# Head sums of six token groups: from selector matmuls on TensorE to copies between SBUF partitions and adds on VectorE

## The chip, the cores and the metric

The kernel runs on one core of one Trainium2 chip. The metric is the time of one execution on the device in microseconds (us). A profiled execution also has a span, from the first to the last instruction, which is about 1.7 us shorter than the time of the same execution. Each profile shows the mean TensorE clock that the chip granted; 1.000 is full speed.

## The reference, cut to what matters

Two layers run over 2048 tokens of width 1024. Each layer has a layer norm, a sliding, dilated attention, a residual, a second layer norm, a dense network with a GELU, and a second residual. The attention has 32 heads of 32 channels; every token looks at itself and at seven earlier tokens, two apart. For each token, head and offset the score is a sum over 32 channels:

```
for offset w in 0..7:
    score[token, head, w] = sum over 32 channels of q[token, head, :] * k[token - 2*(7 - w), head, :]
weights = softmax(score * 32**-0.5)      # over the 8 offsets
out[token, head, :] = sum over w of weights[w] * v[token - 2*(7 - w), head, :]
```

The kernel cuts the tokens into groups of 512. Two layers of four groups make eight groups, numbered 0 to 7. It works as a pipeline: while TensorE does the dense layers of group n, VectorE does the attention of a later group.

Of the kernel before, what the change touches and what calls it, by code (L numbers as in the profile page):

```python
# [9 lines left out]
ALU = mybir.AluOpType  # L10
AX = mybir.AxisListType
BF16 = mybir.dt.bfloat16
F32 = mybir.dt.float32
# [4 lines left out]
def kernel(  # L18
# [18 lines left out]
    P = 128  # L37
    _, S, D = A_x.shape
    F = B_w1.shape[1]
    H = 32  # L40
    DH = D // H
    W = 8
    DIL = 2
    HALO = (W - 1) * DIL
# [3 lines left out]
    T = 512  # L48
    NTT = T // P
# [4 lines left out]
    HP = P // H  # L54
# [18 lines left out]
    bigp = ctx.enter_context(tc.tile_pool(name="bigp", bufs=3))  # L73
    dram = ctx.enter_context(tc.tile_pool(name="dram", bufs=2, space=bass.MemoryType.DRAM))
    smp = ctx.enter_context(tc.tile_pool(name="smp", bufs=1))
# [28 lines left out]
    vec, act, pool, sp = InOrder(nc.vector), InOrder(nc.scalar), InOrder(nc.gpsimd), InOrder(nc.sync)  # L104
# [12 lines left out]
    def mm(*args, **kwargs):  # L117
        return pe(nc.tensor.matmul(*args, **kwargs))  # L118
# [113 lines left out]
    def ln_first():  # L232

        xa[0] = new_xnT()
        vec.on = True
        both = psum.tile([P, 2, KD, P], BF16, name="L", bufs=1)
        stats = {}
# [24 lines left out]
    def win(t_ap):  # L262
        a = t_ap.ap
        assert len(a) == 2 and a[1][0] == 1 and a[1][1] == HALO + T
        return bass.AP(tensor=t_ap.tensor, offset=t_ap.offset, ap=[list(a[0]), [DIL, W], [1, T]])

    st = {n: {} for n in range(N)}
    xa = {}
    xb = {}
# [9 lines left out]
    def head_sum(n, last=True):  # L279

        if "L" not in st[n]:
            st[n]["L"] = psum.tile([P, W, P], F32, name="L", bufs=1)
            start = True
        else:
            start = False
        L = st[n]["L"]
        prod = st[n]["prods"].pop(0)
        for wh in range(2):
            for tb in range(NTT):
                mm(L[tb * H:(tb + 1) * H, wh * 4:(wh + 1) * 4, :], lhsT=smat[:],  # L290
                   rhs=prod[:, wh * 4:(wh + 1) * 4, tb * P:(tb + 1) * P], start=start,
                   stop=last, skip_group_check=True, tile_position=(0, tb * H))

    def new_prod(n, c):

        s = st[n]
        prod = bigp.tile([P, W, T], BF16, name="big")
        vec.tensor_tensor(out=prod[:], in0=s["qT"][:, c, :].unsqueeze(1).to_broadcast([P, W, T]), in1=win(s["kT"][:, c, :]), op=ALU.mult)
        tree = s["prods"]
        tree.append(prod)  # L300
        if c % 2 == 1:
            for _ in range(1 if c % (NCH // s["parts"]) == 1 else 2):
                b = tree.pop()
                vec.tensor_tensor(out=tree[-1][:], in0=tree[-1][:], in1=b[:], op=ALU.add)

    def gen_qkv(n, parts=1, defer=False, qk_pool=None, v_late=False, qk_next=None):
# [46 lines left out]
        if g + 1 < NG:  # L353
            act.copy(vhalo[:], vT[:, :, T:T + HALO])

    def attend(n):

        s = st[n]
        head_sum(n)
        L = s.pop("L")  # L360
        if n % NG == 0:
            vec.tensor_tensor(out=L[0:H, 0:W - 1, 0:HALO], in0=L[0:H, 0:W - 1, 0:HALO], in1=mask[:], op=ALU.add)
        mx = smp.tile([P, P], F32, name="mx")
        vec.tensor_reduce(out=mx[:], in_=L[:].rearrange("p w t -> p t w"), axis=AX.X, op=ALU.max)
        e = smp.tile([P, W, P], F32, name="e")
        vec.tensor_tensor(out=e[:], in0=L[:], in1=mx[:].unsqueeze(1).to_broadcast([P, W, P]), op=ALU.subtract)
        act.activation(e[:], e[:], ACT.Exp, scale=SCALE)
        z = smp.tile([P, P], F32, name="z")
        vec.tensor_reduce(out=z[:], in_=e[:].rearrange("p w t -> p t w"), axis=AX.X, op=ALU.add)
        vec.reciprocal(z[:], z[:])  # L370
        a = smp.tile([P, W, P], BF16, name="a")
        vec.tensor_tensor(out=a[:], in0=e[:], in1=z[:].unsqueeze(1).to_broadcast([P, W, P]), op=ALU.mult)
        s["a"] = a
# [45 lines left out]
    def gen_ffn1(n):  # L419
        xnT = xb.pop(n)  # L420
        hT = hpool.tile([P, KF, T], BF16, name="hT")
        st[("h", n)] = hT
        for j4 in range(KF // 4):
            wt = wpool.tile([P, KD, 4 * P], BF16, name="wt")
            sp.dma_start(wt[:], w1_v[:, :, j4 * 4 * P:(j4 + 1) * 4 * P])
            for jj in range(4):
                j = j4 * 4 + jj
                ps = acc_tile()
                for k in range(KD):
                    mm(ps[:], lhsT=wt[:, k, jj * P:(jj + 1) * P], rhs=xnT[:, :, k, :], start=(k == 0), stop=(k == KD - 1))  # L430
                act.activation(hT[:, j, :], ps[:], ACT.Gelu_apprx_tanh, bias=b1T[:, j:j + 1])
                yield

    def gen_ffn2(n):
        l, g = divmod(n, NG)
        hT = st.pop(("h", n))
        for dh in range(2):
            cols = slice(dh * HALF, (dh + 1) * HALF)
            xb2 = None
            if n == N - 1:  # L440
                xb2 = bigp.tile([P, NTT, HALF], F32, name="big")
                for tt in range(NTT):
                    vec.tensor_tensor(out=xb2[:, tt, :], in0=x[g * NTT + tt][:, cols], in1=b2bc[:, cols], op=ALU.add)

            parts = [[slice(0, HALF)] for _ in range(NTT)]
            if n == N - 1 and dh == 1:
                parts[-1] = [slice(0, HALF // 2), slice(HALF // 2, HALF)]
            pss = [[acc_tile() for _ in p] for p in parts]
            for kq in range(4):
                wt = wpool.tile([P, KQ, HALF], BF16, name="wt")  # L450
                sp.dma_start(wt[:], w2_v[:, kq * KQ:(kq + 1) * KQ, cols])
                for tt in range(NTT):
                    t = g * NTT + tt
                    for ps, cs in zip(pss[tt], parts[tt]):
                        ps = ps[:, 0:cs.stop - cs.start]
                        for k in range(KQ):
                            mm(ps, lhsT=hT[:, kq * KQ + k, tt * P:(tt + 1) * P], rhs=wt[:, k, cs],
                               start=(kq == 0 and k == 0), stop=(kq == 3 and k == KQ - 1))
                        if kq < 3:
                            continue  # L460
                        out_cols = slice(dh * HALF + cs.start, dh * HALF + cs.stop)
                        xs = x[t][:, out_cols]
                        if xb2 is not None:
                            vec.tensor_tensor(out=xs, in0=ps, in1=xb2[:, tt, cs], op=ALU.add)
                        else:
                            tmp = iop.tile([P, HALF], F32, name="tmp")
                            vec.tensor_tensor(out=tmp[:], in0=ps, in1=b2bc[:, out_cols], op=ALU.add)
                            vec.tensor_tensor(out=xs, in0=tmp[:], in1=xs, op=ALU.add)
                        if l == NLAYER - 1:
                            sp.dma_start(out_v[t * P:(t + 1) * P, out_cols], xs)  # L470
                    yield
# [24 lines left out]
    def stage(gen, count=None, sides=()):  # L496


        u = 0
        while count is None or u < count:  # L500
            if next(gen, gen) is gen:
                break
            for v, f in sides:
                if v == u:
                    f()
            u += 1
        for v, f in sides:
            if v >= u:
                f()

    def at(u, f, *args, **kwargs):
        return [(u, lambda: f(*args, **kwargs))]

    def each(f, n, u0, du, c0=0, c1=NCH):
        return [(int(u0 + du * (c - c0)), lambda c=c: f(n, c)) for c in range(c0, c1)]

    hold = vec.hold
# [14 lines left out]
        stage(q2, sides=each(new_prod, 1, 0, 1, 4, 8) + at(4, transpose_late))  # L532
    hpool = ctx.enter_context(tc.tile_pool(name="hpool", bufs=1))
    stage(gen_ffn1(0), sides=at(4, attend, 1) + at(4, spread, 1) + at(4, hold) + each(new_prod, 2, 2, 1, 0, 4) + each(av, 1, 6, 2))
    stage(gen_ffn2(0), sides=at(0, ln_stats_ahead, 3) + at(15, hold) + each(new_prod, 2, 15, 1, 4, 8) + at(23, hold) + at(23, ln_a, 3, None, True))
    for n in range(1, N - 2):
        stage(gen_wo(n), sides=at(0, spread, n + 1) if n > 1 else at(7, attend, 2))
        stage(gen_qkv(n + 2), sides=(at(0, spread, 2) if n == 1 else []) + each(av, n + 1, 0, 2, 0, 3))
        stage(gen_ffn1(n), sides=at(20 if n == 1 else 9, attend, n + 2) + each(av, n + 1, 8, 2, 3, 8))
        if n + 3 < N:  # L540
            stage(gen_ffn2(n), sides=at(2, ln_a, n + 3))
        else:
            stage(gen_ffn2(n), sides=at(0, spread, n + 2) + each(av, n + 2, 1, 4))
    n = N - 2
# [35 lines left out]
```

## The kernel before: the parts that the change and the argument touch

Every instruction of VectorE (DVE), ScalarE (ACT), GpSimd (POOL) and of the weight-load queue is issued through one helper, which the profile therefore names as line L93. All matmuls but the transposes go through `mm`, line L118.

```python
    class InOrder:
        def __getattr__(self, name):
            f = getattr(self.engine, name)
            def call(*args, **kwargs):
                inst = f(*args, **kwargs)                     # L93
                ...                                           # cut: optional order against earlier ones
                return inst
            return call
        def hold(self):                                       # what comes later stays behind what was issued so far
            self.floor = self.last

    vec, act, pool, sp = InOrder(nc.vector), InOrder(nc.scalar), InOrder(nc.gpsimd), InOrder(nc.sync)
    def mm(*args, **kwargs):
        return pe(nc.tensor.matmul(*args, **kwargs))          # L118; `pe` keeps program order
```

TensorE and POOL keep program order. The order of VectorE, ACT and the weight-load queue is chosen when the program is built, apart from the `hold` calls; once built, it is fixed. Six accumulators `acc` in PSUM take the results of TensorE (`bufs=6`); `big` has three buffers.

The 32 channels of a head lie four to a chunk in eight chunks. `new_prod` multiplies q and k for a chunk and VectorE adds the chunks up pairwise, until one product of 128 partitions (32 heads x 4 channels), 8 offsets and 512 tokens is left. `head_sum` adds the last four partitions of each head: a selector matrix `smat` of ones does it on TensorE, in eight matmuls of 128x32, and puts 128-token blocks under each other, so that `L` has (block, head) on the partitions. `attend` does the softmax.

```python
    def head_sum(n, last=True):
        ...
        for wh in range(2):
            for tb in range(NTT):                             # NTT = 4 token blocks, H = 32 heads
                mm(L[tb * H:(tb + 1) * H, wh * 4:(wh + 1) * 4, :], lhsT=smat[:],
                   rhs=prod[:, wh * 4:(wh + 1) * 4, tb * P:(tb + 1) * P], ...)

    def new_prod(n, c):
        prod = bigp.tile([P, W, T], BF16, name="big")
        vec.tensor_tensor(out=prod[:], in0=q of chunk c, in1=win(k of chunk c), op=ALU.mult)   # shortened
        ...                                                   # cut: pairwise adds

    def attend(n):
        head_sum(n)
        L = s.pop("L")
        ...
        vec.tensor_reduce(out=mx[:], in_=L[:].rearrange("p w t -> p t w"), axis=AX.X, op=ALU.max)
        e = smp.tile([P, W, P], F32, name="e")
        vec.tensor_tensor(out=e[:], in0=L[:], in1=mx[:].unsqueeze(1).to_broadcast([P, W, P]), op=ALU.subtract)
        act.activation(e[:], e[:], ACT.Exp, scale=SCALE)
        vec.tensor_reduce(out=z[:], in_=e[:].rearrange("p w t -> p t w"), axis=AX.X, op=ALU.add)
        ...                                                   # cut: reciprocal, a = e * 1/z

    # in gen_qkv, before the V chunks are written:
        act.copy(vT[:, :, 0:HALO], (zhalo if g == 0 else vhalo)[:])      # vT has bufs=2
    # in gen_ffn1, 28 times:
                act.activation(hT[:, j, :], ps[:], ACT.Gelu_apprx_tanh, bias=b1T[:, j:j + 1])
    # the layer norm of the next group, four times: rows to columns by a transposing DMA
        sp.dma_start_transpose(xnT[:, tt, :, :], xn[:].rearrange("s (k p) -> s k p", p=P))
```

The driver issues the stages in this order; `at(u, f)` calls `f` after output tile `u` of the stage.

```python
    stage(gen_ffn2(0), sides=... + at(23, hold) + at(23, ln_a, 3, None, True))
    for n in range(1, N - 2):
        stage(gen_wo(n), sides=at(0, spread, n + 1) if n > 1 else at(7, attend, 2))
        stage(gen_qkv(n + 2), sides=...)
        stage(gen_ffn1(n), sides=at(20 if n == 1 else 9, attend, n + 2) + each(av, n + 1, 8, 2, 3, 8))
        ...                                                   # cut: ffn2 of n, layer norm of n + 3
```

## Time and profile before

| | before |
|---|---|
| time | 1239.21 us median of 3 runs (1239.06 to 1240.82) |
| span of the profiled run, granted clock | 1237.2 us, 1.000 |
| TensorE (PE) busy | 1231.2 us |
| VectorE (DVE) busy | 840.0 us, 68% |
| waits of PE after 150 us | none over 0.45 us |

These are lines of the page of the kernel before: busy time with share of the span, the chain of work that ended last by engine, and the issues of one kind of copy (number, size of each, median us from issue to landing).

```profile
PE 1231.2 (100%) x5841; PEld 632.9 (51%) x5841; DVE 840.0 (68%) x868; ACT 306.3 (25%) x477; POOL 94.3 (8%) x214
...
PE 97%; DVE 1%; POOL 1%; DMA 0%; issue 0%; ACT 0%
...
abc<-a_d POOLq DMA_DIRECT2D x32, 256.0 KB, 4.6
```

PE works nearly the whole time and the chain that decides the end is PE. So only two things can move the time: fewer instructions on PE, or new waits of PE.

### The profile page before, as it was taken

The numbers are of one execution on the slowest core, as the hardware profiler recorded it, in microseconds if no ns is written. First come the engines' busy times: TensorE is split into PE (matmuls) and PEld (weight loads), VectorE is DVE, ScalarE is ACT, GpSimd is POOL, SyncE is SP. The second block draws the span as 40 slices with busy tenths as digits, with TensorE's granted clock in tenths as the row PEclk, the third lists the DMA queues.
The fourth block names the chain that finished last, engine by engine and source line by source line (L and its number), as shares of the span: only waits on it lengthen the run. The fifth ranks groups of instructions, "written<-read, shape, count | busy, mean of one in ns | idle before, by whom it ended". The sixth has DMA issues, their size and how long they took to land.

```text
span 1237.2 us, 14039 instructions
## 1 busy us (share of the span) xinstructions
PE 1231.2 (100%) x5841; PEld 632.9 (51%) x5841; DVE 840.0 (68%) x868; ACT 306.3 (25%) x477; POOL 94.3 (8%) x214
## 2 busy tenths in 40 slices
PE   9999999999999999999999999999999999999998
PEld 6666544456444564445644455444654444444444
DVE  7989899996985899337994379843597788012001
ACT  4333252023420144101341023510235001300310
POOL 4010210012000100001000010100001002000000
PEclk9999999999999999999999999999999999999999
DMA  9954564576646555656556565566654568556441
GB/s 308 279 179 146 165 198 161 168 176 216 191 156 201 161 177 161 196 168 183 170 157 198 172 182 160 164 198 199 171 170 135 184 200 193 169 157 195 152 136 53
DMA packets 215327, 219.81 MB, mean 178 GB/s; under 512 B 66066, under 2 KB 184992, under 8 KB 212192
## 3 DMA queue, kind: packets, MB, share of 16 engines
q1 hardware_dynamic: 212592, 208.16, 54.7%
q0 software_dynamic: 2672, 10.76, 2.8%
q8 instruction: 45, 0.74, 0.2%
q14 instruction: 18, 0.15, 0.0%
HBM read 197.40 MB, written 6.29 MB: 165 GB/s over the span
## 4 chain that ended last, share of the span: by engine, by line
PE 97%; DVE 1%; POOL 1%; DMA 0%; issue 0%; ACT 0%
PE acc L118 97%; POOL rstd L93 1%; DVE stats L93 1%; PE L L118 0%; DVE x L93 0%; DMA x<-in_A_x_dram 0%; DVE xn L93 0%; DVE big L93 0%; PE acc L211 0%; DVE mv L93 0%; PE L L211 0%; ACT xnT L93 0%
## 5 line engine op out<-in xcount | busy, mean ns | idle before, releaser
L118 PE MATMUL acc<-xnT,wt 128*128 128x512 bf16 (+1 forms) x3376 | 721.7, 376 | 0.6 <-ACT xnT L93 0.6
L118 PEld LDWEIGHTS <-wt 128*128 128x128 bf16 x3376 | 398.6, 119 | 320.9 <-issue 3.9
L118 PE MATMUL acc<-wt,hT 128*128 128x512 bf16 (+1 forms) x1820 | 388.1, 376 | 0.0
L118 PEld LDWEIGHTS <-hT 128*128 128x128 bf16 x1820 | 178.1, 98 | 209.0
L93 DVE TENSOR_TENSOR big<-big 128x1024 bf16<-128x1024 bf16 (+2 forms) x184 | 244.2, 1359 | 1.8
L93 ACT ACTIVATE hT<-acc,b1T 128x512 bf16<-128x512 f32 x224 | 151.8, 687 | 319.8 <-PE acc L118 319.2
L93 DVE TENSOR_TENSOR big<-abc,vT 128x4096 bf16<-128x4096 bf16 x64 | 144.0, 2283 | 49.3 <-DMA abc<-a_d 49.3
L93 DVE TENSOR_TENSOR tmp<-acc,b2bc 128x512 f32<-128x512 f32 x56 | 38.6, 690 | 180.9 <-PE acc L118 177.4
L93 DVE TENSOR_TENSOR big<-qT,kT 128x4096 bf16<-128x4096 bf16 x64 | 143.8, 2285 | 23.7 <-ACT kT L93 23.1
L93 ACT CAST qT<-acc 128x512 bf16<-128x512 f32 x64 | 37.4, 586 | 329.2 <-PE acc L118 329.2
L118 PE MATMUL acc<-wt,oT 128*128 128x512 bf16 x448 | 97.9, 379 | 0.0
L93 DVE BATCH_NORM_STATS2 stats<-x 128x6 f32<-128x512 bf16 x128 | 83.7, 679 | 3.3 <-DMA x<-in_A_x_dram 2.7
L118 PEld LDWEIGHTS <-oT 128*128 128x128 bf16 x448 | 43.8, 98 | 52.9 <-issue 0.2
L93 DVE TENSOR_TENSOR x<-acc,big 128x512 bf16<-128x512 f32 (+1 forms) x9 | 5.7, 633 | 90.0 <-PE acc L118 90.0
L93 ACT CAST vT<-acc 128x512 bf16<-128x512 f32 x64 | 37.5, 586 | 83.7 <-PE acc L118 83.7
L93 POOL TENSOR_TENSOR rstd<-mv,eps_t 128x1 f32<-128x1 f32 x60 | 18.5, 308 | 502.3 <-DVE mv L93 502.3
L93 ACT CAST kT<-acc 128x512 bf16<-128x512 f32 x64 | 37.5, 586 | 71.7 <-PE acc L118 71.7
L93 POOL DMA_DIRECT2D a_d<-a x32 | 19.0, 620 | 410.7 <-DVE a L93 410.7
L93 DVE TENSOR_SCALAR xn<-x,mv,rstd 128x1024 bf16<-128x1024 bf16 x52 | 28.6, 550 | 30.0 <-POOL rstd L93 29.5
L93 DVE TENSOR_TENSOR x<-acc,x 128x512 bf16<-128x512 f32 x64 | 43.0, 672 | 6.1 <-PE acc L118 5.8
L93 DVE TENSOR_TENSOR x<-tmp,x 128x512 bf16<-128x512 f32 x56 | 38.6, 690 | 1.5
L93 POOL TENSOR_TENSOR rstd<-rstd,mhalf 128x1 f32<-128x1 f32 x60 | 33.9, 565 | 4.7
(54 smaller groups left out, 211.3 us busy)
## 6 DMA issues: line engine op xcount, KB each, us to landing
wt<-in_B_w_dram SPq DMA_DIRECT2D x56, 1024.0 KB, 5.5
wt<-in_B_w_dram SPq DMA_DIRECT2D x64, 896.0 KB, 4.7
wt<-in_A_wqkv_dram SPq DMA_DIRECT2D x46, 1024.0 KB, 5.6
wt<-in_A_wo_dram SPq DMA_DIRECT2D x16, 1024.0 KB, 4.9
abc<-a_d POOLq DMA_DIRECT2D x32, 256.0 KB, 4.6
x<-in_A_x_dram SPq DMA_DIRECT2D x16, 256.0 KB, 5.4
out_dram<-x SPq DMA_DIRECT2D x31, 128.0 KB, 1.8
wt<-in_A_wqkv_dram SPq DMA_DIRECT2D x4, 512.0 KB, 6.8
```

The lines of the kernel that those rows point to most:

```text
L93: inst = f(*args, **kwargs)
L118: return pe(nc.tensor.matmul(*args, **kwargs))
```

## The change

The intent is to take six of the eight head sums off PE, the engine that bounds the kernel, and to put them on engines with room. Groups 0 and 1 keep the matmuls.

```diff
@@ new_prod: the product is laid out by token block
-        prod = bigp.tile([P, W, T], BF16, name="big")
-        vec.tensor_tensor(out=prod[:], in0=..., in1=win(s["kT"][:, c, :]), op=ALU.mult)
+        prod = bigp.tile([P, NTT, W, P], BF16, name="big")
+        q = s["qT"][:, c, :].rearrange("p (b t) -> p b t", t=P)
+        vec.tensor_tensor(out=prod[:], in0=q.unsqueeze(2).to_broadcast([P, NTT, W, P]), in1=win_by_tile(s["kT"][:, c, :]), op=ALU.mult)
@@ new
+    def gather(n):
+        s = st[n]
+        prod = s["prods"].pop(0)
+        Lq = bigp.tile([P, HP, W, P], BF16, name="big")
+        s["Lq"] = Lq
+        for tb in range(NTT):
+            pool.dma_start(Lq[tb * H:(tb + 1) * H, :, :, :], prod[:, tb, :, :])
@@ attend
-        head_sum(n)
-        L = s.pop("L")
+        e = smp.tile([P, W, P], F32, name="e")
+        if "Lq" in s:
+            Lq = s.pop("Lq")
+            vec.tensor_tensor(out=e[:], in0=Lq[:, 0, :, :], in1=Lq[:, 1, :, :], op=ALU.add)
+            for j in range(2, HP):
+                vec.tensor_tensor(out=e[:], in0=e[:], in1=Lq[:, j, :, :], op=ALU.add)
+            L = e
+        else:
+            head_sum(n)
+            L = s.pop("L")
@@ driver
-    stage(gen_ffn2(0), sides=... + at(23, hold) + at(23, ln_a, 3, None, True))
+    stage(gen_ffn2(0), sides=... + at(23, hold) + at(23, gather, 2) + at(23, ln_a, 3, None, True))
         stage(gen_qkv(n + 2), ...)
+        gather(n + 2)
         stage(gen_ffn1(n), ...)
```

Each of the four copies of a group reads all 128 partitions and writes 32 of them: the four channels of a head, which lay on four partitions, come to lie side by side on one.

More of the change, by code (lines that the diff above doesn't have):

```diff
@@ L265, in win, with win_by_tile @@
         return bass.AP(tensor=t_ap.tensor, offset=t_ap.offset, ap=[list(a[0]), [DIL, W], [1, T]])
+    def win_by_tile(t_ap):
+        a = t_ap.ap
+        assert len(a) == 2 and a[1][0] == 1 and a[1][1] == HALO + T
+        return bass.AP(tensor=t_ap.tensor, offset=t_ap.offset, ap=[list(a[0]), [P, NTT], [DIL, W], [1, P]])
     st = {n: {} for n in range(N)}
@@ L290, in head_sum @@
                 mm(L[tb * H:(tb + 1) * H, wh * 4:(wh + 1) * 4, :], lhsT=smat[:],
-                   rhs=prod[:, wh * 4:(wh + 1) * 4, tb * P:(tb + 1) * P], start=start,
+                   rhs=prod[:, tb, wh * 4:(wh + 1) * 4, :], start=start,
                    stop=last, skip_group_check=True, tile_position=(0, tb * H))
@@ L296, in new_prod @@
         s = st[n]
-        prod = bigp.tile([P, W, T], BF16, name="big")
-        vec.tensor_tensor(out=prod[:], in0=s["qT"][:, c, :].unsqueeze(1).to_broadcast([P, W, T]), in1=win(s["kT"][:, c, :]), op=ALU.mult)
+        prod = bigp.tile([P, NTT, W, P], BF16, name="big")
+        q = s["qT"][:, c, :].rearrange("p (b t) -> p b t", t=P)
+        vec.tensor_tensor(out=prod[:], in0=q.unsqueeze(2).to_broadcast([P, NTT, W, P]), in1=win_by_tile(s["kT"][:, c, :]), op=ALU.mult)
         tree = s["prods"]
@@ L364, in attend @@
         vec.tensor_reduce(out=mx[:], in_=L[:].rearrange("p w t -> p t w"), axis=AX.X, op=ALU.max)
-        e = smp.tile([P, W, P], F32, name="e")
         vec.tensor_tensor(out=e[:], in0=L[:], in1=mx[:].unsqueeze(1).to_broadcast([P, W, P]), op=ALU.subtract)
@@ L534 @@
     stage(gen_ffn1(0), sides=at(4, attend, 1) + at(4, spread, 1) + at(4, hold) + each(new_prod, 2, 2, 1, 0, 4) + each(av, 1, 6, 2))
-    stage(gen_ffn2(0), sides=at(0, ln_stats_ahead, 3) + at(15, hold) + each(new_prod, 2, 15, 1, 4, 8) + at(23, hold) + at(23, ln_a, 3, None, True))
+    stage(gen_ffn2(0), sides=at(0, ln_stats_ahead, 3) + at(15, hold) + each(new_prod, 2, 15, 1, 4, 8) + at(23, hold) + at(23, gather, 2) + at(23, ln_a, 3, None, True))
     for n in range(1, N - 2):
```

## The prediction

> **What bounds the kernel now.** TensorE. The page gives PE 1231.2 us busy of a 1237.2 us span; the chain of waits is 97% PE; the granted clock is 1.000. In the list of waits PE waits for others about 3 us in all, at the start. In mid-kernel an output tile of eight 128x512 matmuls takes 1.727 us (spacing of the ACT evictions in the timeline), without gaps. VectorE is 68% busy (840 us), DMA about 55%, POOL 8%. So only PE instructions removed, or new PE waits, can move the time.
>
> **Removed.** Six of eight head sums, eight 128x32 matmuls each. The chain of waits gives 0.55 us for each. The eviction spacing around those of groups 3 and 4 is 2.38 us instead of 1.73, so each really costs 0.65 us: the column strips overlap (eight separate matmuls would be 1.73), and about 0.1 us is lost around them[...]. 6 x 0.65 = 3.9 us, all on the critical chain; I expect all of it back.
>
> **Added.**
> - VectorE: three adds of 128x1024 with float32 result per group. The trace's float32 `e<-L,mx` of that size takes 1.217 us[...]. 3 x 1.22 = 3.65 us, 22 us in all. Maximum and subtraction now read SBUF: still near 1.22. The product's new layout (inner run 128, not 512) I take as unchanged, 2.29 us.
> - POOL and DMA: four issues per group (0.5 to 0.65 us each) and 1 MB copied. By the `abc<-a_d` issues, also 256 KB, a copy lands after 4.6 us; so the sums' inputs are there 7 to 9 us after the last product.
>
> **Moved.** POOL runs in program order, so the rstd of the next group's first layer norm now stands behind the copy, about 40 us later in a steady iteration; its rows are needed about 100 us later. The copy holds a second of the three slots of `big` for a few us; `av` may wait a little.
>
> **Is it off the critical path?** A steady iteration (152.6 us) has 99 to 106 us of VectorE work; VectorE sits idle 12.8 us before `abc`, then 6.8 and 18.2 us before evictions. The tightest deadline is group 7: its products end at 924 us, the copy lands near 933, when the head sum ran anyway; the softmax ends 4 to 8 us later than 949.7, the last `oT` near 1012 instead of 1006, needed at 1026.5. Group 2's copy is done by about 255 us, before its head sum at 263. PE should see none of it.
>
> **Predicted:** 1239.2 - 3.9 + about 0.3 for small new waits = 1235.6 us, range 1234.0 to 1238.6. Chances: faster by over 2% 0.01, within 2% 0.96, slower by over 2% 0.03.
>
> **What would show it.** Matmuls on `L` fall from 64 to 16 (head sums); evictions near the old head sums at 1.73 us; PE busy about 1227 us, 97% of the chain; new `e` adds near 1.22 us, 18 in all; VectorE about 862 us; copies landing 4 to 6 us after issue; no PE wait over 0.5 us after the start.
>
> **What would make it wrong.** (1) The change shuffles instructions on VectorE, ACT or the SP queue, and PE waits on a late `oT`, `kT` or weight tile: some us, up to tens; likeliest at groups 2 and 3 (VectorE nearly full from 291 to 366 us) or 7. (2) The product's layout falls to half speed: 64 x 2.2 us = 140 us more VectorE work, over 2%. (3) The rstd behind the copy holds a transpose in the SP queue, and weight loads behind it come late.

## More of the kernel before

The timeline of PE in the kernel before, around the stages that matter (start us, duration us, instructions; idle time before would stand in brackets):

```profile
249.03 13.98 PE L118 MATMUL acc<-wt,oT 128*128 128x512 bf16 x64
262.94 0.62 PE L118 MATMUL L<-big,smat 128*32 128x512 bf16 x8
263.49 77.92 PE L118 MATMUL acc<-xnT,wt 128*128 128x512 bf16 x360
...
475.50 31.25 PE L118 MATMUL acc<-xnT,wt 128*128 128x512 bf16 x144
```

There is no bracket: PE runs through. At 249 us it does the output projection of group 1; at 263.5 us it starts q, k and v of group 3, for which it needs all four transposes `xnT<-xn` of group 3.

The groups of instructions of the kernel before, with busy us, mean ns of one, and idle time ahead of them:

```profile
L93 DVE TENSOR_REDUCE z<-e 128x128 f32<-128x1024 f32 x8 | 15.4, 1920 | 2.3 <-ACT e L93 2.3
L93 DVE TENSOR_REDUCE mx<-L 128x128 f32<-128x1024 f32 x8 | 9.7, 1217 | 0.0
L118 PE MATMUL L<-big,smat 128*32 128x512 bf16 x64 | 4.9, 385 | 0.0
```

Sixty-four matmuls are the head sums, eight for each group. Note the two reductions of the same size: `mx` reads `L` in PSUM and takes 1217 ns, `z` reads `e` in SBUF and takes 1920 ns. Both read with a stride.

## The result, and the profile after

| | before | after |
|---|---|---|
| time, runs of the same session | 1239.13 us (6 runs, 1238.64 to 1240.82) | 1239.57 us (6 runs, 1237.95 to 1241.89) |
| ratio | | 1.0002, 95% interval 0.9989 to 1.0015 |
| profiled span, clock | 1237.2 us, 1.000 | 1238.1 us, 1.000 |

A ratio here is the mean time of one kernel's fast runs over that of the other's in the same rounds, so it is not quite the ratio of the medians. The time didn't move, while 3.6 us less had been predicted. The result is numerically correct.

The same lines of the page of the kernel after:

```profile
PE 1224.4 (99%) x5743; PEld 631.7 (51%) x5793; DVE 864.3 (70%) x886; ACT 305.3 (25%) x477; POOL 126.5 (10%) x238
...
PE 59%; DVE 6%; issue 1%; ACT 0%; POOL 0%; DVEq 0%
...
big<-big POOLq DMA_DIRECT2D x24, 256.0 KB, 7.7
```

PE is busy 6.8 us less. Part of that is an artefact: this trace lacks some matmul records (48 matmuls fewer should be 5793, and 5743 are there). The chain now ends differently: the view follows it back only to 423 us. From 504 us to the end it is all PE, which makes the 59%; between 423 and 504 us it runs mostly over VectorE. So something held PE shortly before 504 us; what came before 423 us this line can't tell. VectorE has 24.3 us more, and the new copies took 7.7 us each, not 4.6.

The groups of instructions after:

```profile
L93 DVE TENSOR_TENSOR e<-e,big 128x1024 f32<-128x1024 f32 x12 | 14.5, 1212 | 0.0
L93 DVE TENSOR_REDUCE mx<-e 128x128 f32<-128x1024 f32 x6 | 11.5, 1910 | 0.0
L93 DVE TENSOR_TENSOR e<-big 128x1024 f32<-128x1024 bf16 x6 | 7.3, 1218 | 0.0
L118 PE MATMUL L<-big,smat 128*32 128x512 bf16 x16 | 1.2, 385 | 0.0
```

The adds take 1.21 to 1.22 us as predicted and the head-sum matmuls fell to 16. The product `big<-qT,kT` stayed at 2285 ns. But the maximum, which now reads SBUF, takes 1910 ns instead of 1217 ns, as `z` already did.

The timeline of PE after, in the same stretch:

```profile
249.05 13.98 PE L118 MATMUL acc<-wt,oT 128*128 128x512 bf16 x63
265.76 89.98 PE L118 MATMUL acc<-xnT,wt 128*128 128x512 bf16 x416 [2.73 <-DVE x L93]
355.58 48.51 PE L118 MATMUL acc<-wt,hT 128*128 128x512 bf16 x219
...
504.29 5.34 PE L118 MATMUL acc<-xnT,wt 128*128 128x512 bf16 x24 [1.78 <-ACT hT L93]
```

Here are two new waits, of 2.73 and 1.78 us. Their sum, 4.5 us, is somewhat more than the 3.9 us that the prediction put down for the matmuls. The rest of the document is about these two.

**The first wait** has a misleading name. "DVE x" is what the view puts down as the last releaser, but the work that PE resumes with needs the transposes of group 3. Their single landings in the two traces (read from the records of the issues, us from the span's start) are:

```
                       before                     after
               issued  landed  took      issued  landed  took
transpose 1    246.96  249.72   2.77     246.52  252.44   5.92
transpose 2    248.27  253.00   4.73     247.83  261.43  13.59
transpose 3    249.61  253.81   4.20     249.22  262.19  12.96
transpose 4    252.00  258.25   6.25     253.87  265.62  11.76
copies of group 2                        246.68  252.43   5.75
                                         247.52  253.84   6.31
                                         248.07  260.61  12.54
                                         248.61  261.38  12.76
```

The last transpose landed at 265.62, and PE resumed at 265.76. That it is this landing, and not the VectorE instruction of the view, the other traces show: in all five profiles that have this wait (the changed kernel twice, the halo kernel twice, the copies alone, all below), PE resumed 0.13 or 0.14 us after the last transpose had landed. In the kernel before it landed at 258.25, 5.2 us before PE started on it at 263.49.

The copies reached the fourth transpose in two ways. It took 5.5 us longer, and it was issued 1.9 us later: the rows `xn` lie in three buffers, so VectorE could not write the fourth tile until the first transpose had landed.

```profile
252.54 0.55 DVE L93 TENSOR_SCALAR xn<-x,mv_ahead,rstd_ahead 128x1024 bf16<-128x1024 bf16 x1 [3.01 <-DMA xnT<-xn]
```

The DMA view of the stretch from 243 to 262 us says the same in summary (count, size, median us to landing). Before:

```profile
wt<-in_A_wqkv_dram SPq DMA_DIRECT2D x2, 1024.0 KB, 5.6
xnT<-xn SPq DMA_TRANSPOSE x6, 3.5
```

After:

```profile
wt<-in_A_wqkv_dram SPq DMA_DIRECT2D x2, 1024.0 KB, 8.2
big<-big POOLq DMA_DIRECT2D x4, 256.0 KB, 9.4
xnT<-xn SPq DMA_TRANSPOSE x4, 12.4
```

In this stretch the packets of the queue of the weights and transposes (q1) took 58.8% of the time of 16 DMA engines and those of the queue of the copies (q0) 44.4%; before, the first took 79.1%, and there were none of the second.

**The second wait** is PE waiting for an accumulator that a GELU on ACT has to empty. The timeline of ACT in the kernel before, at the exponential of group 4:

```profile
483.71 1.06 ACT L93 ACTIVATE e<-e 128x1024 f32<-128x1024 f32 x1 [0.83 <-DVE e L93]
484.79 1.28 ACT L93 ACT_TABLE_LOAD   x1
486.08 1.84 ACT L93 ACTIVATE hT<-acc,b1T 128x512 bf16<-128x512 f32 x3
487.81 0.29 ACT L93 COPY vT<-vhalo 128x112 bf16<-128x112 bf16 x1
```

And of the kernel after:

```profile
490.46 0.69 ACT L93 ACTIVATE hT<-acc,b1T 128x512 bf16<-128x512 f32 x1 [1.04 <-PE acc L118]
499.00 0.29 ACT L93 COPY vT<-vhalo 128x112 bf16<-128x112 bf16 x1 [7.85 <-DVE big L93]
...
501.18 1.06 ACT L93 ACTIVATE e<-e 128x1024 f32<-128x1024 f32 x1
502.25 1.28 ACT L93 ACT_TABLE_LOAD   x1
503.55 3.00 ACT L93 ACTIVATE hT<-acc,b1T 128x512 bf16<-128x512 f32 x5
```

Before, ACT stood 0.83 us for the exponential. After, it stands 7.85 us at the copy of the V halo (it waits until VectorE has read an old V buffer for the last time), then does the exponential between two table loads. But for one GELU at 499.19 us (in the cut), the GELUs behind come only at 503.55, and PE, with its six accumulators full, waits. That ACT takes nothing out of turn here is what this trace shows: PE finished another accumulator every 1.73 us, and ACT did nothing for the 7.85 us that it stood at the copy.

What VectorE does for group 4 in that time, in the timeline of the kernel after (the instructions between belong to the attention of group 3):

```profile
486.97 1.22 DVE L93 TENSOR_TENSOR e<-big 128x1024 f32<-128x1024 bf16 x1
...
490.30 1.22 DVE L93 TENSOR_TENSOR e<-e,big 128x1024 f32<-128x1024 f32 x1
...
492.57 1.22 DVE L93 TENSOR_TENSOR e<-e,big 128x1024 f32<-128x1024 f32 x1
...
494.82 1.89 DVE L93 TENSOR_REDUCE mx<-e 128x128 f32<-128x1024 f32 x1
...
498.84 1.20 DVE L93 TENSOR_TENSOR e<-e,mx 128x1024 f32<-128x1024 f32 x1
```

The subtraction ends at 500.04 us. In the kernel before it ran from 482.47 to 483.68 us. Of these 16.4 us, 5.4 were there before group 4's copies began: its products ended at 471.95 us, against 466.57 before (its products started 5.4 us later too, and PE began q, k and v of group 4 1.6 us later). The four copies then took from 472.58 to 485.06. Only 3.65 us are the adds themselves; VectorE's fixed order spreads the sequence over 13 us between other work.

### The profile page after: what moved, and what is told of

It is laid out like the page before. It is cut to its first block, busy times and chain, and to the rows that moved or that the text cites. A ratio compares the mean times of both kernels' runs of the same rounds, so it can differ in the third digit from the quotient of the medians.

```text
span 1238.1 us, 13934 instructions
## 1 busy us (share of the span) xinstructions
PE 1224.4 (99%) x5743; PEld 631.7 (51%) x5793; DVE 864.3 (70%) x886; ACT 305.3 (25%) x477; POOL 126.5 (10%) x238
## 4 chain that ended last, share of the span: by engine, by line
PE 59%; DVE 6%; issue 1%; ACT 0%; POOL 0%; DVEq 0%
PE acc L118 59%; DVE big L93 4%; DVE e L93 0%; DVE stats L93 0%; POOL rstd L93 0%; DVE oT L93 0%; DVE mx L93 0%; ACT L93 0%; DVE xn L93 0%; ACT e L93 0%; ACT hT L93 0%; DVE x L93 0%; DVE mv L93 0%; DVEq L93 0%
## 5 line engine op out<-in xcount | busy, mean ns | idle before, releaser
L93 DVE TENSOR_TENSOR big<-big 128x2048 bf16<-128x2048 bf16 (+2 forms) x184 | 246.2, 1359 | 2.6
L93 DVE TENSOR_TENSOR big<-qT,kT 128x4096 bf16<-128x4096 bf16 x64 | 143.7, 2285 | 26.7 <-ACT kT L93 26.1
L93 POOL TENSOR_TENSOR rstd<-mv,eps_t 128x1 f32<-128x1 f32 x60 | 27.5, 458 | 448.2 <-DVE mv L93 448.1
L93 POOL DMA_DIRECT2D big<-big x24 | 13.7, 577 | 295.8 <-DVE big L93 236.9
L93 POOL TENSOR_TENSOR rstd<-rstd,mhalf 128x1 f32<-128x1 f32 x60 | 43.4, 724 | 4.7
```

## The experiments

Theories to be told apart. **Main theory:** the removal saves about 4 us as predicted, and two new waits give it back; the first comes from the copies of group 2, issued in the same microseconds as the transposes of group 3; the second from ACT's fixed order, in which the halo copy and the exponential of group 4 stand where VectorE isn't ready. **Rivals:** the removal is worth less than predicted; the new product layout costs time; the adds alone or the copies alone do it all; and, for the second wait, that group 3's later softmax pushes everything behind it ("theory F" in the texts below), against group 4's own copies and adds ("G"). The runs of the kernel before in these sessions had medians of 1238.8 to 1239.1 us.

### Nothing but the removal

The head sums are removed, nothing is put in their place, and `attend` reads the product in place. The result is wrong.

```diff
-        Lq = bigp.tile([P, HP, W, P], BF16, name="big")
-        s["Lq"] = Lq
-        for tb in range(NTT):
-            pool.dma_start(Lq[tb * H:(tb + 1) * H, :, :, :], prod[:, tb, :, :])
+        s["Lq"] = prod
...
-            (three adds)
-            L = e
+            L = Lq[:, 0, :, :]
```

> Head sums of groups 2 to 7 removed with nothing in their place (no copies, no adds; the softmax reads one quarter of the product: a wrong result on purpose). Theory A (the removal is worth 6 x 0.65 us and the change gave it back in two new PE waits, near 266 us and near 504 us): 1235.3 us, 3.9 below before, and no PE wait over 0.5 us after the first 150 us. Rival B (the packed head sums cost the kernel less than they seem to, something else bounds it): 1238.5 to 1239.5 us.

Measured: 1234.73 us (1234.67 to 1235.1, 5 runs), ratio 0.9967 (0.9955 to 0.998). No wait of PE after 150 us; where the changed kernel has its first wait, the timeline of PE runs through without a bracket:

```profile
262.64 89.95 PE L118 MATMUL acc<-xnT,wt 128*128 128x512 bf16 x416
```

Against the 1238.93 us of before, the removal is worth 4.2 us, or 0.7 us for each head sum. The size of the saving was right, and the new layout of the product, which this kernel has, costs nothing that shows.

### The adds without the copies

As above, but the adds are kept; they read the product in place (wrong result).

> The three float32 adds per group are kept, but read the product where it lies: no copies (wrong result on purpose). Theory A: the transposes near 247 to 254 us land after 3 to 5 us again, the wait near 266 us is gone; the wait near 504 us is smaller or gone, since the softmax starts earlier: 1235.3 to 1236.5 us. Rival C (the 22 us of added VectorE work are what costs the time): 1238.5 us or more, with PE or ACT waiting for VectorE as in the changed kernel.

Measured: 1239.3 us (1237.36 to 1239.6, 5 runs), ratio 0.9997 (0.9986 to 1.0009). The expectation missed by some 3 us. The first wait is gone, but the second is there, earlier and longer. In the timeline of PE of this kernel:

```profile
488.33 20.84 PE L118 MATMUL acc<-xnT,wt 128*128 128x512 bf16 x88 [2.58 <-ACT hT L93]
```

ACT stood 7.81 us before the exponential of group 4, here after fewer GELUs. And something more came: right after the wait the granted clock (the last but two of the figures in the window view: us, busy us by engine, then clock, DMA share, GB/s) was 0.64, and eight matmuls came at 0.43 us spacing instead of 0.216.

```profile
488.30:493.00 4.70, 4.67 (x14) 1.80 (x14) 4.70 (x5) 3.45 (x6) 0.00 (x0) 0.64 0.00 0
```

The three runs with mean clock 0.998 took 1239.3 to 1239.6 us, the two with 1.000 took 1237.4 us. So a stretch at half clock after the wait cost about 1.9 us on top of it; the wider spacing of the eight matmuls alone makes 1.7. It came after a wait of 2.58 us. Only one of the five runs was profiled; that the two others of the same time and clock had it too, and the two faster ones not, is inferred. The 2.73 us wait in the profile of the changed kernel was not followed by it.

### The copies without the adds

The copies are kept, the adds are not (wrong result).

```diff
-            (three adds)
-            L = e
+            L = Lq[:, 0, :, :]
```

> The changed kernel with its copies but without the three adds (wrong result on purpose), the fourth corner beside before, e1 and e2. Theory A: the first wait stays (it belongs to the copies of group 2), 1 to 6 us; the second shrinks, since group 4's exponential gets its input 4 to 7 us earlier: under 0.5 us. 1236 to 1239 us, with a spread of some us. If the adds make the first wait, the time is that of e1, 1234.7 us.

Measured: 1239.6 us (1239.01 to 1240.44, 5 runs), ratio 1.0007 (0.9993 to 1.0021). The first wait is there, 2.54 us, now named by the timeline as `xnT<-xn`; the clock was 0.69 from 266 to 270 us, and the 416 matmuls behind the wait took 91.44 us, 1.5 more than in the run without copies and adds (89.95). That stretch, which the expectation left out, puts the time just above its range. The second wait is absent, as expected. So the two halves of the replacement each give back about the whole saving, in different places:

| head sums by | time |
|---|---|
| TensorE (before) | 1238.9 us |
| nothing | 1234.7 us |
| adds only | 1239.3 us |
| copies only | 1239.6 us |
| copies and adds (after) | 1239.57 us |

They don't add up, because the waits don't: how long PE waits depends on where ACT stands, and whether the clock halves varies.

### The copies of group 2 eight microseconds later

The copies are issued in the next stage, after the transposes, and not beside them. The arithmetic is unchanged, the result correct.

```diff
-    stage(gen_ffn2(0), sides=... + at(23, hold) + at(23, gather, 2) + at(23, ln_a, 3, None, True))
+    stage(gen_ffn2(0), sides=... + at(23, hold) + at(23, ln_a, 3, None, True))
-        stage(gen_wo(n), sides=at(0, spread, n + 1) if n > 1 else at(7, attend, 2))
+        stage(gen_wo(n), sides=at(0, spread, n + 1) if n > 1 else at(2, gather, 2) + at(7, attend, 2))
```

> As the changed kernel, but the copies of group 2 are issued about 12 us later, behind the first layer norm tile of the output projection of group 1. Theory A (the first PE wait is for the transposed rows of group 3, whose transposes share the DMA engines with the copies and take 12 to 13.6 us): the four transposes land 3 to 5 us after issue, the PE wait at 263 to 266 us falls below 0.5 us, and the kernel takes about 2.5 us less than the changed one: 1237 us. Rival D (PE waits for the VectorE eviction that the list of waits names, because VectorE has more to do): the wait stays over 2 us, 1239.5 us.

Measured: 1237.06 us (1235.91 to 1237.35, 5 runs), ratio 0.9982 (0.9971 to 0.9994), as expected. The transposes of group 3 landed 3.34, 4.47, 3.86 and 6.21 us after issue, about as before the change, and PE doesn't wait at 263 us:

```profile
262.61 89.95 PE L118 MATMUL acc<-xnT,wt 128*128 128x512 bf16 x416
```

The moved copies now slow two transposes of a later set, to 12.2 and 11.4 us, but those are not needed so soon. A second wait of 1.06 us is left at 500 us. So the first wait was caused by the copies of group 2 beside these transposes.

### The halo copy at its place in the program

`hold` on ACT keeps the copy of the V halo behind what was issued ahead of it.

```diff
+        if n > 2:
+            act.hold()
         act.copy(vT[:, :, 0:HALO], (zhalo if g == 0 else vhalo)[:])
```

> As the changed kernel, but the copy of the old V columns into the next vT is held on ACT until its place in the program (no earlier than the K chunks of the same group). Theory A (in the second wait ACT stands in order before an instruction that waits for a late VectorE, the GELUs behind it keep the accumulators full): that copy no longer blocks, but the exponential of group 4 stands there as well and its input comes at 500 us; the PE wait near 504 us falls from 1.8 to about 0.6 us, the time by about 1.1 us: 1238.4 us. If the halo copy alone is the cause, the PE wait goes to 0; if it has no part in it, the wait stays at 1.8 us.

Measured: the second wait fell from 1.78 to 0.69 us, as expected; ACT now stood 5.92 us at the exponential itself. The time did not follow: 1242.12 us (1236.79 to 1242.8, 6 runs), ratio 1.0015 (1.0002 to 1.0029). In the profiled run, the fastest, the first wait was only 0.92 us.

### Two looks again: the changed kernel, and the halo kernel

No edit; one run each, so of unknown state.

> The changed kernel once more, for a second profile: its six runs spread over 4 us, those of the kernel before over 0.8. Theory A: the first PE wait is the landing of the last of four transposes in a crowd of copies and one weight load; its length differs from run to run (0.9 us in the profile of e4, 2.7 in that of the changed kernel), and where it is long TensorE is granted half its clock for a few us after it. This profile shows the wait at 262 to 270 us ending with a transpose landing, 0.9 to 6 us long, and the time is the span of e1 plus both waits. Rival: the runs differ in something else (clock over long stretches, other waits).

> The kernel of e4 once more, whose runs without a profile took 1242 us where the profiled one took 1236.8. Theory A: if this run falls near 1242, the profile shows a first wait of 3 us or more and a stretch at half clock right after it, and the second wait near 0.7 us as before; if it falls near 1237, a first wait near 1 us and no half clock.

Measured: 1242.73 us at clock 0.999, and 1243.31 us at clock 0.997. In the timeline of PE of the changed kernel's second look:

```profile
267.28 91.41 PE L118 MATMUL acc<-xnT,wt 128*128 128x512 bf16 x416 [4.41 <-DMA xnT<-xn]
```

The transposes 2 to 4 took 15.10, 14.43 and 13.18 us here, the last landed at 267.15, and the clock was 0.60 from 266 to 270 us. In the halo kernel's second look the first wait was 5.06 us and the second 0.67 us; the clock was 0.50 from 266 to 270 us and 0.65 from 270 to 274 us. So the first wait varies from run to run: 2.73 and 4.41 us in the two profiles of the changed kernel, 0.92 and 5.06 us in those of the halo kernel. The two longest were followed by half clock: the 416 matmuls behind them took 91.41 and 92.26 us instead of 89.95. This fits the spread of the changed kernel (1237.95 to 1242.73 us, where the kernel before has 1238.5 to 1240.8), and it can hide the shorter second wait of the halo kernel in its median; for the runs without a profile it is not shown. The halo experiment's times therefore settle nothing about the halo; its profiles do.

### What in a copy slows a transpose: bytes, or how they are written

The same 24 copies of 256 KB at the same places, but each writes all 128 partitions (2 KB a partition) and not 32 of them (8 KB a partition). The sums are wrong.

```diff
-            pool.dma_start(Lq[tb * H:(tb + 1) * H, :, :, :], prod[:, tb, :, :])
+            pool.dma_start(Lq[:, tb, :, :], prod[:, tb, :, :])
```

> The changed kernel with the same 24 copies of 256 KB at the same places, but each copy now goes from 128 partitions to the same 128 partitions (2 KB a partition) instead of from 128 partitions to 32 (8 KB a partition); the sums are wrong on purpose. If what slows the four transposes of group 3 is the number of bytes copied beside them, they land 11 to 15 us after issue again, TensorE waits 0.9 to 5 us near 264, and the time is 1238 to 1243 us as for the changed kernel. If it is the way of writing (a copy that fills only 32 partitions), the copies land in about 3 to 5 us each, the transposes in 3 to 7 us, TensorE doesn't wait near 264, and the time is near 1237 us, because the second wait near 500 stays at 0.7 to 1.8 us.

The DMA view of this kernel from 243 to 262 us:

```profile
wt<-in_A_wqkv_dram SPq DMA_DIRECT2D x2, 1024.0 KB, 5.8
big<-big POOLq DMA_DIRECT2D x4, 256.0 KB, 5.4
xnT<-xn SPq DMA_TRANSPOSE x5, 6.7
```

The four transposes of group 3 landed 5.00, 7.55, 6.69 and 6.74 us after issue, and PE didn't wait at 263 us. Over the whole kernel these copies took 3.7 us in the median, where the changed kernel's took 7.7 us for the same bytes. The queue of these copies shows it too (packets, MB, share of the time of 16 DMA engines). In the changed kernel, then here:

```profile
q0 software_dynamic: 4592, 17.05, 6.0%
...
q0 software_dynamic: 4592, 17.05, 4.3%
big<-big POOLq DMA_DIRECT2D x24, 256.0 KB, 3.7
```

The time was 1235.96 us (1235.89 to 1236.36, 4 runs), ratio 0.9977 (0.9961 to 0.9994), 1 us less than expected; a second wait of 0.95 us was still there, at 487 us. So it is mainly the form of the destination, not the number of bytes. The bytes may count for something: three of the four transposes took 2 to 3 us longer than in the kernel before. Why a copy into 32 partitions takes 7.7 us and one into 128 takes 3.7 us was not shown. Nor does any run here settle why transposes beside a copy into 32 partitions take 10 to 15.5 us. One pattern is in the traces: in the five profiles with the first wait, the second transpose landed 0.03 to 0.12 us after the last of the four copies, as if it had to wait for them.

### The head sum of group 3 back on TensorE

The later copies of group 2 as above, and group 3 keeps the head sum on PE.

```diff
-        gather(n + 2)
+        if n != 1:
+            gather(n + 2)
```

> As e3 (copies of group 2 issued later), and group 3 has its head sum on TensorE again (five groups changed). Theory F (the second PE wait, near 500 us, begins at group 3: its softmax ends near 385 instead of 366 us, so its value products fall into a stretch where VectorE is full, group 4's products start 4 to 5 us late and ACT stands before group 4's halo copy and exponential): the group 3 softmax ends near 366 to 370 us, the PE wait near 500 us is under 0.3 us, and the time is before less 5 x 0.65: 1235.7 us. Rival G (group 4's own copies and adds make that wait): it stays at 1 us or more, 1236.8 us or more.

Measured: 1243.94 us (1243.6 to 1245.48, 5 runs), ratio 1.0045 (1.0031 to 1.0058), clock 0.997 in all. The expectation missed. The timeline of PE:

```profile
346.89 1.04 PE L118 MATMUL L<-big,smat 128*32 128x512 bf16 x8 [5.85 <-DVE big L93]
```

PE keeps program order, and it came to the head sum before the products of group 3 were done; the clock was 0.60 from 346 to 352 us. The products ended at 346.8 us, where the kernel before had them at 338.2 us for a head sum at 341.3 us. So a head sum on PE is itself a place where PE can be held, and before the change only 3.2 us of slack kept it from that. Near 500 us no wait over 0.45 us is left, but PE was shifted by then, so this run is inconclusive for the second wait.

### The head sum of group 4 back on TensorE

The same with group 4 instead of group 3 (`if n != 2`).

> As e3, and group 4 instead of group 3 has its head sum on TensorE again. Theory F: group 4's products still start late (436 us or later instead of 432.5), ACT still waits some us for the exponential's input, and the PE wait only shrinks: 0.3 to 1 us left, 1236 to 1236.7 us. Rival G: the wait is gone, 1235.7 us.

Measured: 1235.38 us (1235.25 to 1235.79, 5 runs), ratio 0.9972 (0.9959 to 0.9984); no wait of PE after 150 us. One group left unchanged is enough to lose the second wait, although group 3 is still done the new way, and although group 4's products still ended late, at 470.2 us (466.57 in the kernel before, where PE began q, k and v of group 4 even 1.6 us later). So the lateness that comes from group 3 isn't enough; group 4's own copies and adds are needed for the second wait.

### The softmax of group 3 earlier

The later copies of group 2, and `attend` of group 3 at tile 14 of its stage instead of 20.

```diff
-        stage(gen_ffn1(n), sides=at(20 if n == 1 else 9, attend, n + 2) + ...)
+        stage(gen_ffn1(n), sides=at(14 if n == 1 else 9, attend, n + 2) + ...)
```

> As e3, and the softmax of group 3 stands earlier in the program (unit 14 instead of 20), so VectorE takes it before the last value products of group 2; nothing else is changed and no work taken away. Theory F: it ends near 368 to 372 us, group 4's products start near 433 us, the PE wait near 500 us falls from 1.1 to under 0.5 us, 1235.3 us. If lateness of group 3 has no part in the wait, it stays near 1.1 us: 1236.5 us.

Measured: 1238.46 us (1237.77 to 1240.92, 5 runs), ratio 1.0001 (0.9988 to 1.0013). The second wait stayed at 0.83 us, against 1.06 us, and a new one came up at 383 us, 2.70 us, named `tmp`: the reordered VectorE now emptied accumulators of another stage too late. The clock was 0.72 from 383 to 389 us. But the edit did not do what it was meant to: the softmax of group 3 ended at 381.6 us and not at 368 to 372, and group 4's products started at 439.0 us, as long after PE had begun q, k and v of group 4 as without the edit (19.2 us). So this run does not test theory F; the run before, with group 4 on TensorE, is what speaks against it. Moving work blindly can make the next wait.

### Both waits taken away

The later copies of group 2, the halo copy at its place, and the exponential of group 4 held until tile 21 of its stage, so that VectorE has finished when ACT comes to it.

```diff
+    # the copies of group 2 in gen_wo(1), and act.hold() before the halo copy, as above
+        s["e"] = e
+        if n != 4:
+            attend_end(n)
+
+    def attend_end(n):
+        s = st[n]
+        e = s.pop("e")
+        if n == 4:
+            act.hold()
         act.activation(e[:], e[:], ACT.Exp, scale=SCALE)
...
+        + (at(21, attend_end, 4) if n == 2 else [])          # among the sides of gen_ffn1
```

> As e3, and on ACT both the V halo copy (as in e4) and group 4's exponential are put behind later GELUs (22 of the stage instead of 16), so ACT stands in front of no late VectorE result while evictions wait. Theory A: both PE waits are gone, all of the removal is kept: before less 3.9 to 4.2, 1235.0 us, no PE wait over 0.3 us after 150 us. If PE waits at 500 us for something else than ACT's order: 1236.5 us as e3.

Measured: 1235.12 us (1234.74 to 1235.49, 5 runs), ratio 0.9969 (0.9956 to 0.9981), correct, clock 1.000. The line of ACT that answers to the ones above:

```profile
496.82 1.06 ACT L93 ACTIVATE e<-e 128x1024 f32<-128x1024 f32 x1 [0.58 <-DVE e L93]
```

VectorE is as late with the subtraction as in the run with the later copies alone (496.8 and 496.7 us), but ACT stands 0.58 us instead of 7.85 us, and PE doesn't wait after 150 us. The line of PE at the place of the second wait has no bracket:

```profile
414.62 89.95 PE L118 MATMUL acc<-xnT,wt 128*128 128x512 bf16 x416
```

This version has all six groups changed and beats both kernels: it keeps 3.8 of the 4.2 us, as expected. As it contains both remedies, it shows that the two waits are nearly the whole loss, not what each is worth; for the first that is the run with the later copies.

## Why the prediction was wrong, point by point

- **What bounds the kernel: right.** PE was the chain, and taking only its matmuls away moved the time by 4.2 us (predicted 3.9).
- **The cost of the adds and the layout: right.** 1.21 to 1.22 us for an add, 2285 ns for the product as before, VectorE at 864.3 us (predicted 862).
- **"Maximum and subtraction now read SBUF: still near 1.22": half wrong.** The subtraction takes 1.215 us, the maximum 1.910 us. The trace of before had the evidence: the strided reduction `z<-e` from SBUF stood at 1920 ns beside `mx<-L` at 1217 ns. A cost should be taken from the instruction with the same source and the same access pattern.
- **"A copy lands after 4.6 us": wrong.** It was taken from `abc<-a_d` of equal size, but took 7.7 us in the median, and the last of a group's four landed 10.2 to 14.7 us after the first was issued (predicted 7 to 9 us after the last product). The run with spread destinations shows that filling only 32 partitions makes most of the difference (3.7 us in the median).
- **The step that failed: "PE should see none of it", and in the list of signs "no PE wait over 0.5 us after the start".** The prediction looked for a deadline of the copied data and found slack. It didn't ask what the copies do to transfers of others: at group 2 they were issued between the four transposes of group 3, which had 5.2 us of slack, and made them land 2.7 to 8.4 us later, the last one 7.4 us; PE then waited 2.73 us. Nor did it ask where ACT stands in its fixed order while VectorE's chain to the exponential gets 16 us later; six full accumulators then hold PE, for 1.78 us. The tightest deadline was named at group 7; it was at groups 3 and 4.
- **The list of what would make it wrong: point (1) named the right class,** a wait of PE by the order on VectorE, ACT or the weight-load queue, with groups 2 and 3 as likely places, though not the tiles: PE waited for transposed rows and for an empty accumulator, not for `oT`, `kT` or weights. It was then given 0.3 us in the sum and little weight in the range. Point (2), the layout, didn't happen (2285 ns as before). Point (3) foresaw late transposes, but the cause was the copies on the DMA engines, not the rstd behind them on POOL: only delaying the copies of group 2 restored the transposes (3.34 to 6.21 us).
- **A cost that wasn't thought of:** after most of its waits of 2.5 us and more PE ran at half clock for a while (granted clock 0.50 to 0.72 in the stretches read behind them); in the run with adds alone that was about 1.9 us, nearly as much as the wait again. After 150 us the kept profiles hold seven waits of PE of 2.5 us or more. Six of them, from 2.54 to 5.85 us, were followed by a stretch at half clock that cost 1.5 to 2.3 us; the one of 2.73 us was not, and none of those up to 1.78 us was. What decides it was not found.

The sum for the profiled run: its span is 5.1 us above that of the run without copies and adds (1238.1 against 1233.0), and the two waits make 4.5 of them; 0.2 us were already there at 249 us. The second look of the changed kernel has a span 8.0 us above it (1241.0): 4.41 and 1.77 us of waits and 1.5 us of half clock (91.41 us for the 416 matmuls behind the first wait instead of 89.95) make 7.7 of them.

Open: why a copy into 32 partitions takes longer than one into 128 (7.7 against 3.7 us); why transposes beside copies into 32 partitions take 10 to 15.5 us, and land hardly before the last of these copies does; what makes the first wait vary from run to run; what decides whether the clock halves; and that groups 5 to 7 don't wait is a matter of slack that no run has tested.

## What to carry to other kernels

When work leaves the engine that bounds a kernel, price not only the new instructions but what they delay: list the transfers that are in flight in the same microseconds and their slack, and for every engine with a fixed order ask which instruction would stand at its head if its input came 10 us later, and whose buffers lie behind it. In this kernel a copy that writes 32 partitions slowed the transfers beside it much more than one that writes all 128 (the second to fourth transposes of group 3 took 9.8 to 15.5 us beside the first kind, all four 5.0 to 7.6 us beside the second); so where the result allows it (here it did not: the sums were wrong), let a copy write all 128 partitions, or issue it where no tight transfer runs. If a gain of a few us vanishes, look first for two or three new waits of the bounding engine; here, moving one group's copies, one halo copy and one exponential brought it back.
